# RetNet attention and SwiGLU block: where the attention's first piece, masks and ticks stand in the order of work

## The chip, the core and the metric

The kernel runs on one core of a Trainium2 chip. The core has five engines with queues of their own, each worked off in order: TensorE (PE, matmuls, with its weight loads shown as PEld), VectorE (DVE), ScalarE (ACT), GpSimd (POOL) and SyncE (SP), which here only issues DMAs. The metric is the device time of one execution in microseconds (us). Before the change it is 1050.05 us, the median of six runs from 1048.7 to 1053.18.

## What is computed

Eight batches of eight heads attend over 576 tokens of 64 values each. The scores are scaled, multiplied by a power of a decay per head where the key is not later than the query, and applied to the values, with no softmax. The result, put side by side by heads, is a matrix x of 4608 tokens by 512 that goes through a SwiGLU block. All is float32.

```python
scores = scale * np.matmul(q, k.transpose(0, 1, 3, 2))
Dmat = np.where(rel >= 0, gamma[:, None, None] ** rel[None, :, :], 0.0)
attn = np.matmul(scores * Dmat[None], v)
x = attn.transpose(0, 2, 1, 3).reshape(4608, 512)
g = x @ w_gate                      # 512 -> 1536
out = (g / (1.0 + np.exp(-g)) * (x @ w_val)) @ w_out   # 1536 -> 512
```

## The kernel before, in words

**The block.** The tokens are cut into five tiles: tile 0 of 512 tokens, tiles 1 to 4 of 1024. In tiles 1 to 4 the products are made by a fast scheme with fewer multiplications, written out by hand in the tables `UP`, `DOWN` and `OUT_SUMS` (L50 to L133): 26 products instead of 32. One line of `UP` is one step: sums of blocks of x, sums of blocks of weights, a product, and then reads of the product's bank (copies, sums, and outputs through silu). A tile's up part is three passes over the 26 lines (one for each 512 columns of the hidden layer), each step four matmuls of 128x256; its down part is one pass over the 26 lines of `DOWN`, six matmuls each. `up_step` (L966) and `down_step` (L1019) emit a step; `reads` (L906) emits what follows the matmuls, on DVE where a bank in PSUM is read, on POOL or DVE else. Line 18 of `UP` has six reads, the most of all. In tile 1 the sums of the weights are made too, by POOL (`w_sums`, L945), and stored by ACT's queue (L986); later tiles fetch them again through SP's queue (`fetch`, L875).

**The attention.** A tick t (L673) works on three pairs of heads at once: on PE it emits the values of pair t-2 (`own_values`, L523, and `earlier_values`, L545), the states of pair t-1 (`new_states`, L536) and the scores of pair t-1 (`scores`, L561). The rest of its work, for DVE and ACT, is put into the list `pieces` and handed out between later steps:

- `copies` (L582): even states out of PSUM on ACT; `own` (L578): the mask on the scores, DVE; `pairs` (L587): the mask on the last chunk's scores (`ret_last`, L589, DVE) and the first of the state sums; `odd`, `evens`: the other state sums, DVE.
- `outputs` (`to_x`, L606): the finished values of pair t-2 are copied into x, by ACT for pairs 8 to 19 (`light`, L451), by DVE for others.
- `keys` (L493) scales k, and `scale_q` (L482) scales q, both on ACT; two transposes on DVE make qT and kT of pair t (L489); `next_load` (L1079) then issues the loads of pair t+2 on SP (13 DMAs or fewer).

Where pair t-2 is light, the list is: copies, outputs and own in one piece; then pairs, odd, and evens with keys, one at a time; then qT; then kT with the loads. `part_on` (L733) hands out one of these behind an up step, unless that step or the next has five reads or more (L1016: so behind steps 17 and 18 none). A down step hands out three pieces (`go_on(3)`, L1053), where the three of pairs, odd and evens count as one. A tick first hands out whatever the last one has left.

**The order.** All engines work in the order in which the program emits (L1062). Ticks 0 to 13 belong to tile 0. `spread_tick` (L1135) places the others among the steps. In tile 1 the first up pass has no tick. Among the 52 steps of the other two passes, `merge` (L1056) spreads six ticks (12 to 17) evenly: ahead of steps 0, 9, 17, 26, 35 and 43. Ticks 18 to 21 stand ahead of the down steps 2, 7, 13 and 19 (L1156). Tile 2 has eight ticks and tile 3 four, spread evenly; tile 4 has none.

Of the kernel before, what the change touches and what calls it, by code (L numbers as in the profile page):

```python
# [17 lines left out]
ALU = mybir.AluOpType  # L18
# [136 lines left out]
def kernel(  # L155
# [32 lines left out]
    nc = tc.nc  # L188
# [386 lines left out]
    def masked(i):  # L575
        p, sr, (ret, ret_last, state) = i % HP, last_scores(i), places(i)

        def own():  # L578
            nc.vector.tensor_tensor(out=ret, in0=sc, in1=near[:, 2 * p : 2 * p + 2].unsqueeze(2).to_broadcast([P, 2, NFULL, L]),
                                    op=ALU.mult)  # L580

        def copies():  # L582
            (nc.vector.tensor_copy if vector(i + 1) else nc.scalar.copy)(out=even, in_=z[:, 0])

        odd_states = state[:, 1:].rearrange("p (c r) d -> p c r d", r=2)[:, :, 1]

        def pairs():  # L587

            nc.vector.tensor_tensor(out=ret_last, in0=sr, in1=last_near[:, p], op=ALU.mult)  # L589
            at = odd_states  # L590
            nc.vector.scalar_tensor_tensor(out=at, in0=even, scalar=step[:, p : p + 1], in1=z[:, 1], op0=ALU.mult, op1=ALU.add)

        def odd():
            at = odd_states
            for c in range(1, NFULL):
                nc.vector.scalar_tensor_tensor(out=at[:, c], in0=at[:, c - 1], scalar=step[:, HP + p : HP + p + 1],
                                               in1=at[:, c], op0=ALU.mult, op1=ALU.add)

        def evens():
            at = state[:, 0 : NC - 1].rearrange("p (c r) d -> p c r d", r=2)  # L600
            nc.vector.scalar_tensor_tensor(out=at[:, :, 1], in0=at[:, :, 0], scalar=step[:, p : p + 1], in1=even,
                                           op0=ALU.mult, op1=ALU.add)

        return [copies, own, [pairs, odd, evens]]

    def to_x(i):  # L606
        b, p = divmod(i, HP)
# [65 lines left out]
    def tick(t, lo=HP, hi=NP, spread=False, then=None):  # L673
        go_on(len(pieces))
        if hi == HP:

            if lo <= t - 1 < hi:
                scores(t - 1, True)
                new_states(t - 1)
                pieces.extend(masked(t - 1))  # L680
                go_on(3)
            if lo <= t - 2 < hi:
                own_values(t - 2)
            for f in transposes(t) if lo <= t < hi else ():
                f()
            if t + 1 == HP:
                split(0)
            if lo <= t - 2 < hi:
                earlier_values(t - 2)
                if t == HP:  # L690
                    rounding(2)
                    rounding(3)
                to_x(t - 2)[0]()
            if t + 1 == HP:
                rounding(0)
            return
        if lo <= t - 2 < hi:
            own_values(t - 2)
        if lo <= t - 1 < hi:
            new_states(t - 1)  # L700
        if lo <= t - 2 < hi:
            earlier_values(t - 2)
        if lo <= t - 1 < hi:
            scores(t - 1, t - 2 < lo)
        if lo <= t - 1 < hi and whole(t - 2) and not whole(t - 1):
            decay(slice(0, H), slice(0, H), half[1])
        copies, *masks = masked(t - 1) if lo <= t - 1 < hi else (lambda: None,)
        keys, *new = transposes(t) if lo <= t < hi else (lambda: None,)
        outputs = to_x(t - 2)[0] if lo <= t - 2 < hi else lambda: None
        late = needed(1) - 4 <= t < needed(1) - 2 or light(t - 2)  # L710
        if late and masks:
            own, (pairs, odd, evens) = masks
            pieces.extend([lambda: (copies(), outputs(), own()), [pairs, odd, lambda: (evens(), keys())]])
        elif late:
            pieces.append(lambda: (copies(), outputs(), keys()))
        else:
            pieces.extend([lambda: (copies(), keys()), outputs])
            pieces.extend(masks)
        if then and new:
            pieces.extend(new[:-1])  # L720
            pieces.append(lambda: (new[-1](), then()))
        else:
            pieces.extend(new)
            pieces.extend([then] if then else [])
        if not spread:
            go_on(len(pieces))

    def go_on(n):
        for _ in range(min(n, len(pieces))):
# [236 lines left out]
    def up_step(n, qd, i):  # L966
        label, opens, xslot, _, wslot, _, ops = up[i]
        busy = n == 1
        if qd == 0:
            done = lambda i: X_FIRST + (min(3 * i, 2 * i + 2, i + 6) if busy else i)  # L970
            x_sums(n, done(i), done(i + 1), busy)
        if busy:
            if i > 1:
                w_sums(qd, i)
            w = up_view(qd)(wslot)
        else:
            w = operand()[:, 0:512].rearrange("p (g x) -> p g x", g=2)
        rhs = x_view(n)(xslot)
        b = bank(label, i == 0)
        for gv in range(2):  # L980
            for c in range(2):
                m = nc.tensor.matmul(b[:, gv * TB : (gv + 1) * TB], w[:, gv, ts(c, P)], rhs[:, c, :],  # L982
                                     start=(opens and gv == 0 and c == 0), stop=(c == 1), skip_group_check=True)
        stepped.append(m)
        if busy:
            nc.scalar.dma_start(out=up_ops[qd][i].rearrange("p (g x) -> p g x", g=2), in_=w)  # L986
            if i in (20, 23) and qd + 1 < NQ:
                first_sums(qd + 1, *((0, 2) if i == 20 else (2, 4)))
            if i == 24 and qd + 1 < NQ:
                negated(qd + 1, 1)  # L990
                w_sums(qd + 1, 1)
            if 0 < i < N - 1:
                negated(qd, i + 1)
            if qd + 1 == NQ:
                for _ in range({21: 3, 22: 2, N - 1: 3}.get(i, 0)):
                    fetch()
        else:
            fetch()

        def result(o, src, negative, vector):  # L1000
            s = io[:, (silus[0] % 4) * TB : (silus[0] % 4 + 1) * TB]
            silus[0] += 1
            nc.scalar.activation(out=s, in_=src[:, 0:TB], func=AF.Silu, scale=-1.0 if negative else 1.0)  # L1003
            dst = hid[:, qd, o // 4, o % 4]
            if negative:
                return lambda: nc.vector.scalar_tensor_tensor(out=dst, in0=src[:, TB : 2 * TB], scalar=-1.0, in1=s,  # L1006
                                                              op0=ALU.mult, op1=ALU.mult)
            if vector:
                return lambda: nc.vector.tensor_tensor(out=dst, in0=src[:, TB : 2 * TB], in1=s, op=ALU.mult)
            nc.gpsimd.tensor_tensor(out=dst, in0=src[:, TB : 2 * TB], in1=s, op=ALU.mult)  # L1010

        reads(ops, b, busy, result, i > N // 2)
        if qd + 1 == NQ and i + 1 == N:
            while products:
                products.pop(0)[1]()
        if max(len(line[-1]) for line in up[i : i + 2]) < 5:  # L1016
            part_on()

    def down_step(n, i):  # L1019
# [20 lines left out]
        if n + 1 == NTILE and i + 1 == N:  # L1040
            _, o, a = ops.pop()
            d, t = divmod(int(o), 4)
            at, rows = part[int(a)], starts[n] + t * TB
            assert ops == [["add", a, "b", a]]
            for m, queue in enumerate((nc.sync, nc.scalar)):
                nc.vector.tensor_tensor(out=at[:, ts(m, TB)], in0=b[:, ts(m, TB)], in1=at[:, ts(m, TB)], op=ALU.add)
                queue.dma_start(out=out[rows + m * P : rows + (m + 1) * P, d * TB : (d + 1) * TB], in_=at[:, ts(m, TB)])
            return
        reads(ops, b, False, result)
        at = 2 * (i - (N - 1 - X_FIRST // 2))  # L1050
        if 0 <= at < X_FIRST and n + 1 < NTILE:
# [82 lines left out]

    def spread_tick(t):  # L1135
        tick(t, FIRST, NP, True, lambda: next_load(t))

    ticks = lambda a, b: [lambda t=t: spread_tick(t) for t in range(a, b)]
    for n in range(1, NTILE):
# [10 lines left out]
                                      mybir.DependencyInfo(mybir.DependencyClass.Sync, mybir.DependencyReason.DATA), reason="loads in turn")  # L1150
                    load(FIRST + i // 14)
        downs = [lambda i=i: down_step(n, i) for i in range(N)]
        merge((0.0, ticks(done, cut)), (0.5, ups))
        if n == 1:

            for i, f in reversed(list(zip((2, 7, 13, 19), ticks(cut, upto), strict=True))):  # L1156
                downs.insert(i, f)
            merge((0.5, downs))
        else:
            merge((0.0, ticks(cut, upto)), (0.5, downs))  # L1160
        done = upto

# [29 lines left out]
```

## Time and profile before

| | |
|---|---|
| median of six runs | 1050.05 us (1048.7 to 1053.18) |
| the profiled execution | 1051.12 us, its span 1049.4 us |
| PE, DVE, POOL, ACT busy | 98%, 62%, 38%, 28% of the span |
| tile 1: first up step; first down step | 176.4 us; 327.4 us |
| tile 2, first up step | 412.8 us |
| ticks 14, 15, 16, 17 begin on PE | 253.2, 271.6, 293.3, 309.5 us |
| ticks 18, 19, 20, 21 begin on PE | 332.9, 352.3, 371.9, 389.9 us |

All times within the execution are from the start of the span. A line such as "L489 DVE" is line 489 of the kernel below. A wait "A <- B" is idle time of A that B ended; "issue" is a wait for nothing that the profile shows. Timeline rows give start, duration, engine, line, operation, output<-inputs, shape and count, and in brackets the idle time ahead and what ended it. Equal rows may be merged, and their durations then added or spanned. Rows on windows give, for a stretch, the busy time and the number of instructions of PE, PEld, DVE, ACT and POOL, then the granted clock of PE (1.00 is full), the share of the DMA engines and GB/s.

### The profile page before, as it was taken

To read this page: it belongs to the slowest core of one execution; us is meant where nothing else is said; L and a number is where in the kernel's file an instruction comes from. 1 tells how busy PE (TensorE), PEld (TensorE's weight loads), DVE (VectorE), ACT (ScalarE), POOL (GpSimd) and SP (SyncE) were. 2 spreads that over 40 slices of the span, in tenths; PEclk is the share of its full clock that TensorE was granted. 3 is DMA by queue.
4 is the path that set the end of the run, shared out by engine and by line. 5 is a ranking of instruction groups with operands and counts; after the bars stand their busy time and mean duration, and the time that the engine had idled before them with its cause. 6 is when DMAs were issued, how large, how long until landed. Compare 5 with 4: busy or idle time off the path is not lost.

```text
span 1049.4 us, 21507 instructions
## 1 busy us (share of the span) xinstructions
PE 1030.2 (98%) x8448; PEld 846.3 (81%) x8448; DVE 645.5 (62%) x1063; ACT 294.7 (28%) x646; POOL 401.7 (38%) x347
## 2 busy tenths in 40 slices
PE   6999999999999999999999999999999999999998
PEld 5444555888787888888888888888888888888887
DVE  5668868677668767554467787526376645244644
ACT  4466423242533322132322102223120022231110
POOL 2002367766476016622124048412250483222505
PEclk9999999999999999999999999999999999999999
DMA  9999868776678778755676877445554565555553
GB/s 243 253 276 261 194 201 273 203 208 169 186 206 231 212 194 258 198 149 171 185 205 156 231 176 224 154 141 151 151 180 137 156 193 156 153 151 160 182 161 100
DMA packets 310380, 199.10 MB, mean 190 GB/s; under 512 B 220168, under 2 KB 254984, under 8 KB 310280
## 3 DMA queue, kind: packets, MB, share of 16 engines
q1 hardware_dynamic: 279000, 161.51, 56.0%
q10 hardware_dynamic: 31280, 36.22, 10.2%
q8 instruction: 67, 1.10, 0.4%
q14 instruction: 33, 0.27, 0.1%
HBM read 157.56 MB, written 40.11 MB: 188 GB/s over the span
## 4 chain that ended last, share of the span: by engine, by line
PE 79%; DVE 2%; issue 1%; ACT 0%; DMA 0%; ACTq 0%; DVEq 0%
PE bankC L982 12%; PE bankE L982 12%; PE bankB L982 12%; PE bankA L982 12%; PE bankA L1028 6%; PE bankC L1028 6%; PE bankB L1028 6%; PE bankE L1028 6%; PE outer L531 1%; PE inner L572 1%; PE outer L558 1%; PE inner L542 1%; DVE rest L919 1%; DVE rest L785 0%; DVE arena L1006 0%
## 5 line engine op out<-in xcount | busy, mean ns | idle before, releaser
L919 POOL TENSOR_TENSOR rest<-rest 128x512 f32<-128x512 f32 x65 | 91.7, 1416 | 298.9 <-DVE rest L919 279.9
L1003 ACT ACTIVATE io<-rest 128x256 f32<-128x256 f32 x180 | 74.9, 416 | 320.6 <-DVE rest L919 268.1
L982 PE MATMUL bankC<-rest,arena 128*128 128x256 f32 x544 | 129.0, 380 | 0.0
L982 PE MATMUL bankA<-rest,arena 128*128 128x256 f32 x544 | 128.7, 379 | 0.0
L785 POOL TENSOR_TENSOR arena<-arena 128x512 f32<-128x512 f32 (+1 forms) x72 | 112.1, 1569 | 40.1 <-DMA up<-arena 21.9
L982 PE MATMUL bankE<-rest,arena 128*128 128x256 f32 x512 | 123.2, 384 | 0.6 <-DVE rest L919 0.6
L982 PE MATMUL bankB<-rest,arena 128*128 128x256 f32 x512 | 121.3, 380 | 0.0
L1010 POOL TENSOR_TENSOR arena<-rest,io 128x256 f32<-128x256 f32 x72 | 51.9, 726 | 166.9 <-ACT io L1003 166.9
L982 PEld LDWEIGHTS bankA<-rest,arena 128*128 128x128 f32 x544 | 103.2, 190 | 14.5 <-issue 0.5
L982 PEld LDWEIGHTS bankC<-rest,arena 128*128 128x128 f32 x544 | 102.9, 190 | 14.4 <-POOL arena L785 0.3
L982 PEld LDWEIGHTS bankE<-rest,arena 128*128 128x128 f32 x512 | 97.7, 192 | 15.2 <-DVE rest L919 1.0
L982 PEld LDWEIGHTS bankB<-rest,arena 128*128 128x128 f32 x512 | 97.4, 191 | 13.4
L785 POOL TENSOR_TENSOR rest<-rest 128x256 f32<-128x256 f32 (+1 forms) x66 | 67.6, 1044 | 101.7 <-DVE rest L419 62.0
L919 DVE TENSOR_TENSOR rest<-bankB,rest 128x512 f32<-128x512 f32 x72 | 48.9, 687 | 67.4 <-PE bankB L982 45.1
L919 DVE TENSOR_TENSOR rest<-bankC,rest 128x512 f32<-128x512 f32 x72 | 48.8, 686 | 65.8 <-PE bankC L982 45.9
L919 DVE TENSOR_TENSOR rest<-bankA,rest 128x512 f32<-128x512 f32 x72 | 48.9, 687 | 61.7 <-PE bankA L982 44.3
L919 DVE TENSOR_TENSOR rest<-bankE,rest 128x512 f32<-128x512 f32 x71 | 48.2, 687 | 62.0 <-PE bankE L982 47.0
L1006 DVE SCALAR_TENSOR_TENSOR arena<-rest,io 128x256 f32<-128x256 f32 x84 | 58.2, 695 | 10.9 <-ACT io L1003 10.8
L1028 PE MATMUL bankC<-arena 128*128 128x256 f32 x252 | 59.8, 388 | 0.0
L1028 PE MATMUL bankA<-arena 128*128 128x256 f32 x252 | 58.0, 380 | 1.3 <-DVE arena L785 1.3
L1028 PE MATMUL bankB<-arena 128*128 128x256 f32 x252 | 58.5, 381 | 0.0
L1028 PE MATMUL bankE<-arena 128*128 128x256 f32 x252 | 57.9, 379 | 0.0
(189 smaller groups left out, 1625.5 us busy)
## 6 DMA issues: line engine op xcount, KB each, us to landing
arena<-up SPq DMA_DIRECT2D x234, 256.0 KB, 2.6
arena<-dn SPq DMA_DIRECT2D x104, 384.0 KB, 3.4
up<-arena ACTq DMA_DIRECT2D x78, 256.0 KB, 4.0
dn<-rest SPq DMA_DIRECT2D x78, 128.0 KB, 1.8
out_dram<-rest SPq DMA_DIRECT2D x31, 256.0 KB, 5.3
qk<-in_q_dram SPq DMA_DIRECT2D x108, 72.0 KB, 2.8
qk<-in_k_dram SPq DMA_DIRECT2D x108, 72.0 KB, 2.5
rest<-in_moe_w_out_dram ACTq DMA_DIRECT2D x6, 1024.0 KB, 5.4
```

Of the source, the lines that this page charges most:

```text
L531: m = nc.tensor.matmul(value(i, hl, c), s["v"][rows, at], ret[rows, c % 2 if whole(i) else hl, c // 2], start=start, stop=start, skip_grou ...
L542: nc.tensor.matmul(z[half[hl], r, c], s["kn"][chunk(i, hl, 2 * c + r, i < HP)], s["v"][rows, at], start=True, stop=True, skip_group_check= ...
L558: nc.tensor.matmul(xr[half[hl]] if c + 1 == NC else value(i, hl, c), state[half[hl], c, :], s["qT"][half[hl], column(i, hl, c)], start=Fal ...
L572: nc.tensor.matmul(sc[chunk(i, hl, 2 * c + r)[0], r if whole(i) else hl, c], kT[half[hl], at], qT[half[hl], at], start=True, stop=True, sk ...
L785: eng.tensor_tensor(out=dst, in0=srcs[0], in1=srcs[1], op=ALU.add if op[0] == "add" else ALU.subtract)
L919: eng.tensor_tensor(out=at(op[1]), in0=at(op[2]), in1=at(op[3]), op=ALU.add if op[0] == "add" else ALU.subtract)
L982: m = nc.tensor.matmul(b[:, gv * TB : (gv + 1) * TB], w[:, gv, ts(c, P)], rhs[:, c, :], start=(opens and gv == 0 and c == 0), stop=(c == 1 ...
L1003: nc.scalar.activation(out=s, in_=src[:, 0:TB], func=AF.Silu, scale=-1.0 if negative else 1.0)
L1006: return lambda: nc.vector.scalar_tensor_tensor(out=dst, in0=src[:, TB : 2 * TB], scalar=-1.0, in1=s, op0=ALU.mult, op1=ALU.mult)
L1010: nc.gpsimd.tensor_tensor(out=dst, in0=src[:, TB : 2 * TB], in1=s, op=ALU.mult)
L1028: nc.tensor.matmul(b[:, m * TB : (m + 1) * TB], lhs[:, qd, ts(m, P)], w[:, qd], start=(opens and qd == 0 and m == 0), stop=(qd == NQ - 1), ...
```

## The change

Three things change. `ret_last` leaves `pairs` and becomes a function `last`; in ticks with light values both masks (`own`, `last`) now stand ahead of `outputs`. For ticks from `spread_tick`, the first piece is handed out in the step that follows the tick, between its matmuls and its reads (`after_tick`). And in tile 1 the ticks stand ahead of other steps: 0, 10, 17, 24, 34 and 44 of the two up passes and 4, 8, 14 and 18 of the down part. Tiles 2 and 3 keep their places.

```diff
+        def last():
+            nc.vector.tensor_tensor(out=ret_last, in0=sr, in1=last_near[:, p], op=ALU.mult)
+
         def pairs():
-            nc.vector.tensor_tensor(out=ret_last, in0=sr, in1=last_near[:, p], op=ALU.mult)
             at = odd_states
...
-        return [copies, own, [pairs, odd, evens]]
+        return [copies, own, [last, pairs, odd, evens]]
...
         if late and masks:
-            own, (pairs, odd, evens) = masks
-            pieces.extend([lambda: (copies(), outputs(), own()), [pairs, odd, lambda: (evens(), keys())]])
+            own, (last, pairs, odd, evens) = masks
+            pieces.extend([lambda: (copies(), own(), last(), outputs()), [pairs, odd, lambda: (evens(), keys())]])
         elif late:
             pieces.append(lambda: (copies(), outputs(), keys()))
         else:
             pieces.extend([lambda: (copies(), keys()), outputs])
-            pieces.extend(masks)
+            for own, (last, pairs, *rest_of) in [masks] if masks else []:
+                pieces.extend([own, [lambda: (last(), pairs()), *rest_of]])
...
+    fresh = []
+
+    def after_tick():
+        if fresh:
+            fresh.pop()
+            go_on(1)
...
+        after_tick()
         reads(ops, b, busy, result, i > N // 2)          # up_step
...
+        after_tick()
         reads(ops, b, False, result)                     # down_step
...
     def spread_tick(t):
         tick(t, FIRST, NP, True, lambda: next_load(t))
+        fresh.append(t)
...
-        merge((0.0, ticks(done, cut)), (0.5, ups))
         if n == 1:
-            for i, f in reversed(list(zip((2, 7, 13, 19), ticks(cut, upto), strict=True))):
+            for i, f in reversed(list(zip((0, 10, 17, 24, 34, 44), ticks(done, cut), strict=True))):
+                ups.insert(i, f)
+            merge((0.5, ups))
+            for i, f in reversed(list(zip((4, 8, 14, 18), ticks(cut, upto), strict=True))):
                 downs.insert(i, f)
             merge((0.5, downs))
         else:
+            merge((0.0, ticks(done, cut)), (0.5, ups))
             merge((0.0, ticks(cut, upto)), (0.5, downs))
```

## The prediction

> **What bounds the kernel now.** I read the page first, then the list of waits on TensorE (PE), then the clock in windows of 3.41 us around each wait, and last the timeline and the DMA rows at those places.
>
> ```profile
> span 1049.4 us, 21507 instructions
> PE 1030.2 (98%) x8448; PEld 846.3 (81%) x8448; DVE 645.5 (62%) x1063; ACT 294.7 (28%) x646; POOL 401.7 (38%) x347
> ```
>
> PE is the bound, so only what PE waits for can be won. The columns of the next view are total us, times, longest.
>
> ```profile
> PE inner L572 <- issue: 2.0, 1, 2.0
> PE outer L566 <- DVE kT L489: 1.7, 1, 1.7
> PE bankA L1028 <- DVE arena L785: 1.3, 1, 1.3
> PE bankE L982 <- DVE rest L919: 0.6, 1, 0.6
> ```
>
> All four lie in tile 1, at 337, 275, 366 and 193 us; the other waits in that list fall in tile 0's attention, and from 412 us on there is none. Two of the four cost twice, as windows of activity show (PE busy first, the granted clock after POOL):
>
> ```profile
> 272.66:276.07 3.41, 1.68 (x85) 1.48 (x75) 3.31 (x7) 0.94 (x3) 1.44 (x2) 1.00 0.12 34
> 276.07:279.49 3.42, 3.42 (x9) 2.71 (x9) 0.43 (x1) 0.09 (x2) 0.00 (x0) 0.50 0.99 222
> ...
> 334.10:337.51 3.41, 1.38 (x72) 1.17 (x63) 3.41 (x2) 0.00 (x0) 3.33 (x2) 1.00 0.67 108
> 337.51:340.92 3.41, 3.41 (x11) 2.79 (x9) 1.46 (x1) 0.00 (x0) 3.04 (x2) 0.50 1.08 260
> ...
> 364.82:368.23 3.41, 2.07 (x10) 1.50 (x9) 3.38 (x5) 0.00 (x0) 0.00 (x0) 1.00 0.03 9
> 368.23:371.60 3.37, 3.37 (x17) 2.98 (x16) 2.73 (x4) 0.58 (x1) 0.00 (x0) 1.00 0.82 133
> ```
>
> A window with PE busy 1.68 or 1.38 of 3.41 us is followed by one at clock 0.50, which loses 1.7 us; one with 2.07 us is not. So the wait at 275 cost 1.73 + 1.7 = 3.4 us, that at 337 cost 2.03 + 1.8 = 3.8 us (the step behind it took 4.37 us for the usual 2.59), and that at 366 only 1.3 us. Together 8.5 us: no more can be won here.
>
> **The change part by part.** I write "step" for an up or down step; its PE time is 1.73 us (up) or 2.59 us (down), from the starts in the timeline.
>
> *Tick 15, from step 26 to step 24 (counted from the second pass of tile 1).* Its scores need the kT of tick 14, which a piece of that tick makes. The timeline of before:
>
> ```profile
> 256.47 0.69 DVE L919 TENSOR_TENSOR rest<-bankB,rest 128x512 f32<-128x512 f32 x1 [1.16 <-POOL rest L919]
> ...
> 260.44 2.91 DVE L1006 SCALAR_TENSOR_TENSOR arena<-rest,io 128x256 f32<-128x256 f32 x2
> ...
> 264.69 0.68 DVE L579 TENSOR_TENSOR ret<-inner,near 128x512 f32<-128x512 f32 x1
> ...
> 268.10 1.89 PE L982 MATMUL bankA<-rest,arena 128*128 128x256 f32 x8
> ...
> 273.03 0.77 DVE L489 STREAM_TRANSPOSE qT<-qk 128x576 f32<-128x576 f32 x1
> ...
> 274.31 0.76 DVE L489 STREAM_TRANSPOSE kT<-qk 128x576 f32<-128x576 f32 x1
> ...
> 275.12 0.27 PE L566 MATMUL outer<-qT,kT 64*64 64x64 f32 x2 [1.73 <-DVE kT L489]
> ```
>
> PE ran step 24 at 268.10, tick 15 at 271.64, and wanted kT at 275.12 - 1.73 = 273.39. VectorE (DVE) was some 5 us behind, since steps 18 to 23 read much and each of its SBUF-only operations (L1006) ended only with the POOL sum beside it. Tick 14 stays ahead of step 17. Steps 17 and 18 carry no pieces (step 18 has six reads), so before, the pieces stood behind steps 19 to 24, kT last. After, the first piece is out at step 17 and the rest stand behind 19 to 23: kT moves up by one step. But tick 15 moves up by two. It starts where step 24 did, about 268.15, and wants kT 1.75 us later, at 269.9.
>
> When is kT there? Behind step 23's reads qT ended at 273.80; kT follows it directly, 0.70 later: 274.5. The mask and last mask leave this stretch (0.61 + 0.13, start to start): 273.8. They go where DVE idled before 257.48, but the mask waits for the copy on ScalarE (ACT), which stands behind the silu at 257.20 to 257.61: mask 258.0, last mask 258.6, step 17's read at 258.7 for 257.48: +1.2. DVE's wait of 0.99 for a silu at 272.36 shrinks, as the key scaling stands one step earlier; I take 0.4 of it. So 274.6, a wait of 4.7 us, and a slow window, 1.7: 6.4 against 3.4, **+3.0 us**. Low end: the 1.2 vanishes in waits for POOL and all of the 0.99 goes: 272.8, wait 2.9 and half a slow window 0.9: +0.4. High end: one more L1006 waits out a POOL sum (1.0): 275.6, wait 5.7 and a window and a half, 2.6: +4.9. I take +3.0, the value nearest to the rows.
>
> *Tick 18, from down step 2 to 4.* Its wait is not for an engine: 27 of 30 equal matmuls ran, then 2.03 us nothing. The DMA rows of 334 to 335 us:
>
> ```profile
> q1 hardware_dynamic: 1132, 0.14, 88.4%
> q8 instruction: 1, 0.02, 6.6%
> ```
>
> One packet of instructions of 16 KB (6.6% of 16 engines in 1 us is 1.06 us) travels among 1132 small packets of SyncE's (SP) loads of q and k. I read the wait as PE out of instructions. The loads, of attention tick 19, are issued behind kT of tick 17 (330.87) and take SP from 330.93 to 337.33, over tick 18 at 332.88. After, that kT stands behind step 23, and the loads start 1 to 3 us earlier while tick 18 starts 5.2 us later, at about 338: they no longer meet. **-3.8 us**; the other bound is 0, if PE runs short at another tick. I take -3.8, as the ticks at 293 and 372 us show no such wait. On SP the moved loads (ten DMAs, 6.4 us) also stand ahead of the operands for down steps 5 to 7: issued by 334 and landing in the 6.0 us of the DMA rows there, 340, against down step 5 at about 342.6. If that cover goes, each us late is a us on PE.
>
> *Tick 19, from down step 7 to 8.* The 1.3 us at 366 is down step 11 waiting for the four sums of step 8 (L785, 0.96 each), which stood behind tick 19's DVE work. They now stand ahead of it. But a down step runs three pieces, and with the first already out both transposes follow in the same step, so the sum of step 9, which step 12 needs, stands behind the whole tick: by the same durations it ends near 364 against 363.1 wanted. Late next is step 12, 0.9 us: **-0.4 us**, from -1.3 to +1.0.
>
> *Masks ahead of the copies to x.* In tile 1's down steps the last mask waited for ACT's copies (0.96 us each). Now ACT's copies wait for DVE's masks, and behind them on ACT queue silus, bank copies and key scaling. The next tick writes those banks 10 us later or more, so copies of 1.3 to 1.8 us are hidden; without that cover, about 1 us a tick. ACT is 28% busy. 0. In tile 0 (ticks 10 to 13) a 0.21 us operation moves: 0, within 0.3.
>
> *First piece early in the other ticks.* Ticks 16 and 17 have kT ready 5 steps ahead. At tick 17 the masks fit into DVE's idle 3.04 us before 313.83. In tiles 2 and 3 the piece is copy and key scaling, 1.3 us on ACT, and PE waits for nothing there: 0. The mask build on POOL (1.26 us at 390.27) comes a step earlier into 47 us of POOL idle: 0.
>
> **Sum:** +3.0 - 3.8 - 0.4 = -1.2 us. The profiled execution took 1051.12 us, 1.72 beyond its span; this gives 1049.9. It was 1.07 above the median of the six runs, 1050.05: it fell into both slow windows, which by where a window begins another run can miss. Against the median I see no change. About 0.2% (2.1 us) is what a measurement of this kernel can tell from none.
>
> A rule that speaks here: the Trainium skill, "TensorE: Matmul & The Clock Gate", Part 1, has the clock halve after an idle window of about 3.4 us. The trace differs: 1.7 us idle within a window was enough. By the rule neither wait of before would have cost a slow window, but the new one of 4.7 us could; the sum would be (4.7 + 1.7 - 1.73) - 2.03 - 0.4 = +2.2, an estimate. I go by the rows.
>
> **Rivals.**
>
> Faster: kT is in time. If DVE does not fall 5 us behind, because masks done early let it past steps 18 to 23 without the POOL sums in its way, kT comes by 272: a wait of 2.0, a window 1.7, +0.3. With -3.8 and -1.3 this is 1046.3. For it: 2.9 us of DVE's lag are waits and lock-outs that need not recur. Against: the bare operations from step 18's read at 259.2 on add up to 10.6 us, 269.8, with no wait at all, and POOL is busy until 268.4.
>
> Slower: PE still runs out of instructions once. For it: loads follow each kT directly, ticks 19 and 21 now stand 4 down steps behind the tick whose pieces issue them, and loads of before crossed ticks 17 and 19 unharmed, so that the meeting alone does not decide. At the same 3.8 us the sum is +3.0 - 0.4 = +2.6: 1053.7; it turns the sign from a loss of 2.3 us on, a stop long enough to bring a slow window. Against: one tick out of ten was hit before, and the worst meeting is taken apart.
>
> Slower by tick 15 alone: kT after 276.8 (wait 6.9, window 1.7) is where it outweighs the rest; at 277.2, 1052.6, with a second slow window 1053.5.
>
> The change does not do what it says: the early piece waits for the scores anyway and DVE orders the rest as before, so each wait comes back at its size, 1051.
>
> **How the numbers follow.** Trade of one wait for another, as summed: 0.32. Does nothing: 0.07. Faster: 0.26, widened beyond what the sum gives since the largest term rests on a queue of DVE that I moved by hand. Instructions late: 0.22. Tick 15 alone: 0.13. So within 0.2%: 0.39, faster 0.26, slower 0.35. Predicted 1049.9, its own range 1048 to 1052. The range over the cases reaches from 1045.9, below the faster case, to 1054.0, above the dearest of the slower ones.
>
> **What would show it.** Right: a wait of PE for kT at the scores of tick 15 near 270, longer than 1.73, and a window at clock 0.50 behind it; no wait for "issue" at a tick of the down steps; a short wait at down step 12. Wrong: no wait for kT (then faster), an "issue" wait at any tick (then slower), any wait beyond 412 us.

## The result, and the profile after

The changed kernel takes 1052.14 us in the median of 35 runs (1049.25 to 1057.2), against 1049.07 us for 77 runs of the kernel before, run in turn with it. The ratio is 1.0031, 95% interval 1.002 to 1.0042: slower by about 3 us. A second comparison gave 1.0029 (1.0017 to 1.0042). The prediction was 1049.9 us, with "Against the median I see no change".

The profiled execution took 1051.01 us, almost the 1051.12 of before, so these two profiles taken alone would show no loss. The page of the changed kernel:

```profile
span 1049.3 us, 21500 instructions
PE 1028.1 (98%) x8448; PEld 843.8 (80%) x8448; DVE 654.4 (62%) x1063; ACT 297.6 (28%) x646; POOL 401.3 (38%) x347
```

The list of waits on PE of the changed kernel (total us, times, longest). Lines have moved by 10 behind the new functions: L929 is the old L919, L992 the old L982, L795 the old L785, L1039 the old L1028.

```profile
PE outer L566 <- DVE kT L489: 3.1, 1, 3.1
PE inner L542 <- ACT kn L506: 1.5, 2, 1.3
PE bankC L992 <- DVE rest L929: 1.4, 1, 1.4
...
PE bankE L992 <- DVE rest L929: 1.0, 1, 1.0
PE outer L558 <- DVE state L603: 1.0, 1, 1.0
...
PE bankB L1039 <- issue: 0.2, 1, 0.2
```

The two waits of before in the down part are gone (2.03 us of "issue" at tick 18, 1.3 us at down step 11). The 0.20 us of "issue" left there stand at down step 12 (369.03 us) and are a wait for DVE: a sum (L795) that step 12 needs ended at 368.93. At tick 15, 1.73 us became 1.29 us for the scaled keys kn and 3.11 us for kT. New and not predicted is the 1.4 us for bankC, at step 24 of the third up pass (329 us). The 1.0 us for bankE lies in the first pass, where before had 0.6.

The timeline at tick 15 of the changed kernel (start, duration, engine, line, operation, output<-inputs, shape, count, idle time ahead):

```profile
256.64 0.69 DVE L579 TENSOR_TENSOR ret<-inner,near 128x512 f32<-128x512 f32 x1 [1.62 <-ACT even L583]
257.25 0.21 DVE L588 TENSOR_TENSOR ret_last<-outer,last_near 128x64 f32<-128x64 f32 x1
...
258.06 0.69 DVE L929 TENSOR_TENSOR rest<-bankA,rest 128x512 f32<-128x512 f32 x1 [0.59 <-PE bankA L992]
...
265.15 2.75 DVE L598 SCALAR_TENSOR_TENSOR state<-state,tab 128x64 f32<-128x64 f32 x3
...
270.06 1.08 PE L542 MATMUL inner<-v,kn 64*64 64x64 f32 x29 [1.29 <-ACT kn L506]
...
271.34 0.78 DVE L489 STREAM_TRANSPOSE qT<-qk 128x576 f32<-128x576 f32 x1 [0.58 <-ACT qk L486]
...
274.29 0.77 DVE L489 STREAM_TRANSPOSE kT<-qk 128x576 f32<-128x576 f32 x1
...
275.11 0.37 PE L566 MATMUL outer<-qT,kT 64*64 64x64 f32 x2 [3.11 <-DVE kT L489]
```

The masks do stand early, in DVE's idle time, as the first two rows show. But kT ends at 275.06, where it ended before too (274.31 + 0.76), while PE, held up by kn first, asked for it at 272.00 instead of 273.39. The three `odd` sums of 128x64 take 2.75 us from first start to last end, for 1.50 before: the last two take 1.19 us each, and each ends 0.08 us after a sum of POOL that ran beside it.

Windows of 3.41 us there and at the wait in the third pass (PE, PEld, DVE, ACT, POOL busy with counts, PE's clock, DMA share, GB/s):

```profile
268.71:272.12 3.41, 1.88 (x89) 1.54 (x84) 2.83 (x7) 3.20 (x9) 0.00 (x0) 1.00 0.42 147
272.12:275.53 3.41, 0.42 (x14) 0.42 (x18) 2.94 (x4) 0.42 (x1) 2.67 (x2) 0.50 0.27 88
275.53:278.95 3.42, 3.42 (x38) 2.85 (x33) 0.82 (x2) 1.51 (x5) 0.00 (x0) 0.50 0.67 109
...
326.73:330.14 3.41, 1.97 (x10) 1.44 (x9) 3.41 (x6) 1.47 (x4) 0.98 (x1) 1.00 0.79 297
```

Two windows at clock 0.50 stand at tick 15 in this execution. The first falls mostly on idle time; the second is full of work at half speed.

To compare kernels I cut tile 1 in two, by starts in the timeline: "up" from the first up step of tile 1 to its first down step, "down" from there to the first up step of tile 2. Tiles 2 to 4 take 636.6 to 637.5 us in every profile of this study, so nothing changed there.

| profile | up | down | sum | profiled execution |
|---|---|---|---|---|
| before | 151.05 | 85.32 | 236.37 | 1051.12 |
| before_2 | 149.25 | 83.64 | 232.89 | 1045.22 |
| before_3 | 151.68 | 85.33 | 237.01 | 1051.12 |
| after | 156.60 | 79.96 | 236.56 | 1051.01 |
| after_2 | 156.14 | 79.96 | 236.10 | 1051.8 |
| after_3 | 156.84 | 79.95 | 236.79 | 1056.74 |
| after_4 | 158.92 | 79.97 | 238.89 | 1056.98 |

By the means, with after_4 left out of the up part (4.14 us of it are a wait at 196 us, told of below), the up part lost 5.9 us and the down part gained 4.8. The first of the three up passes has no tick, and its waits differ from profile to profile, from 0.3 to 4.1 us. The other two passes together take 102.7 to 105.2 us in the profiles of before (mean 104.3) and 108.0 to 110.9 us in the four of the changed kernel (mean 109.6).

### The profile page after: what moved, and what is told of

It reads as the page before. It is cut to its first block, busy times and chain, and to the rows that moved or that the text cites. A ratio compares the mean times of both kernels' runs of the same rounds, so it can differ in the third digit from the quotient of the medians.

```text
span 1049.3 us, 21500 instructions
## 1 busy us (share of the span) xinstructions
PE 1028.1 (98%) x8448; PEld 843.8 (80%) x8448; DVE 654.4 (62%) x1063; ACT 297.6 (28%) x646; POOL 401.3 (38%) x347
## 4 chain that ended last, share of the span: by engine, by line
PE 79%; DVE 2%; issue 0%; DMA 0%; ACT 0%; POOL 0%; ACTq 0%; DVEq 0%; POOLq 0%
PE bankC L992 13%; PE bankE L992 12%; PE bankA L992 12%; PE bankB L992 12%; PE bankB L1039 7%; PE bankC L1039 6%; PE bankE L1039 6%; PE bankA L1039 6%; PE outer L531 1%; PE inner L572 1%; DVE rest L929 1%; PE outer L558 1%; PE inner L542 1%; DVE state L598 1%; DVE arena L1016 0%
## 5 line engine op out<-in xcount | busy, mean ns | idle before, releaser
L929 POOL TENSOR_TENSOR rest<-rest 128x512 f32<-128x512 f32 x65 | 91.9, 1418 | 297.4 <-DVE rest L929 276.3
L992 PE MATMUL bankC<-rest,arena 128*128 128x256 f32 x544 | 129.0, 380 | 1.6 <-DVE rest L929 1.4
L992 PE MATMUL bankA<-rest,arena 128*128 128x256 f32 x544 | 130.0, 382 | 0.0
L795 POOL TENSOR_TENSOR arena<-arena 128x512 f32<-128x512 f32 (+1 forms) x72 | 112.5, 1575 | 45.5 <-DMA up<-arena 30.1
L992 PE MATMUL bankE<-rest,arena 128*128 128x256 f32 x512 | 121.4, 380 | 1.0 <-DVE rest L929 1.0
L992 PE MATMUL bankB<-rest,arena 128*128 128x256 f32 x512 | 121.3, 380 | 0.0
L992 PEld LDWEIGHTS bankC<-rest,arena 128*128 128x128 f32 x544 | 102.9, 190 | 16.6 <-issue 1.8
L992 PEld LDWEIGHTS bankA<-rest,arena 128*128 128x128 f32 x544 | 104.1, 192 | 14.9 <-issue 0.5
L992 PEld LDWEIGHTS bankE<-rest,arena 128*128 128x128 f32 x512 | 97.0, 190 | 14.7 <-DVE rest L929 1.4
L992 PEld LDWEIGHTS bankB<-rest,arena 128*128 128x128 f32 x512 | 96.9, 190 | 13.4 <-issue 0.2
L795 POOL TENSOR_TENSOR rest<-rest 128x256 f32<-128x256 f32 (+1 forms) x66 | 66.9, 1035 | 101.2 <-DVE rest L419 61.2
L929 DVE TENSOR_TENSOR rest<-bankC,rest 128x512 f32<-128x512 f32 x72 | 48.9, 688 | 64.7 <-PE bankC L992 45.7
L929 DVE TENSOR_TENSOR rest<-bankB,rest 128x512 f32<-128x512 f32 x72 | 48.8, 686 | 62.9 <-PE bankB L992 48.6
L929 DVE TENSOR_TENSOR rest<-bankA,rest 128x512 f32<-128x512 f32 x72 | 48.9, 687 | 62.4 <-PE bankA L992 45.1
L929 DVE TENSOR_TENSOR rest<-bankE,rest 128x512 f32<-128x512 f32 x71 | 48.2, 688 | 63.3 <-PE bankE L992 49.3
L1016 DVE SCALAR_TENSOR_TENSOR arena<-rest,io 128x256 f32<-128x256 f32 x84 | 56.0, 667 | 10.9 <-ACT io L1013 10.9
L1039 PE MATMUL bankB<-arena 128*128 128x256 f32 x252 | 58.3, 381 | 0.0
L1039 PE MATMUL bankC<-arena 128*128 128x256 f32 x252 | 58.1, 380 | 0.0
L1039 PE MATMUL bankA<-arena 128*128 128x256 f32 x252 | 57.9, 379 | 0.0
L1039 PE MATMUL bankE<-arena 128*128 128x256 f32 x252 | 57.9, 379 | 0.0
```

What stands on the lines that cost most here:

```text
L795: eng.tensor_tensor(out=dst, in0=srcs[0], in1=srcs[1], op=ALU.add if op[0] == "add" else ALU.subtract)
L929: eng.tensor_tensor(out=at(op[1]), in0=at(op[2]), in1=at(op[3]), op=ALU.add if op[0] == "add" else ALU.subtract)
L1039: nc.tensor.matmul(b[:, m * TB : (m + 1) * TB], lhs[:, qd, ts(m, P)], w[:, qd], start=(opens and qd == 0 and m == 0), stop=(qd == NQ - 1), ...
```

## The experiments

Two theories stood at first. One: tick 15's place, two steps earlier, carries the loss. Its rival: the pieces (early first piece, masks ahead) lose time wherever they run, and the place is a detail. A third came up on the way: that the order of the masks costs in tile 0.

**Tick 15 back to step 26, the rest of the change kept.**

```diff
-(0, 10, 17, 24, 34, 44), ticks(done, cut)
+(0, 10, 17, 26, 34, 44), ticks(done, cut)
```

> The changed kernel with one number undone: tick 15 ahead of step 26 again, not 24. Theory (the place of tick 15 is the loss: it leaves no step between the transposes of tick 14 and the scores that need them): the waits of 1.3 and 3.1 us at tick 15 shrink to under 1 us together, no or one slow window instead of two, so 5 to 7 us less than the changed kernel, ratio to the kernel before 0.996 to 0.999. Rival (the early piece pushes VectorE's reads of steps 17 and 18 back): the changed kernel's loss stays, 1.002 to 1.003.

Ratio to before 0.9992 (0.9973 to 1.0012); up 150.37, down 79.96. Its waits on PE in the second and third pass:

```profile
PE bankC L992 <- DVE rest L929: 1.5, 1, 1.5
PE bankA L992 <- DVE rest L929: 0.9, 1, 0.9
PE outer L566 <- DVE kT L489: 0.5, 1, 0.5
```

One number takes the whole loss away. The wait for kT falls to 0.51 us, for the 1.73 of before at the same place. But 0.87 us of that is PE coming later, by a wait for bankA ahead of the tick: together 1.39 us for 1.73.

**Tick 15 at step 25.** The same line with 25.

> The changed kernel with tick 15 ahead of step 25, half of the way back (24 gave an up stretch of 156.6 us, 26 gave 150.4). Theory (time of kT is fixed by VectorE, each step that tick 15 comes earlier is 1.73 us more of waiting): waits at tick 15 of 2.5 to 3 us together, one slow window, up stretch 152.5 to 154.5. Rival (a threshold, the transposes find a free queue or not): as with 24 or as with 26, within 0.7 us.

Up 152.06, down 79.98, one execution of 1051.98 us.

```profile
PE outer L566 <- DVE kT L489: 2.2, 1, 2.2
...
PE bankC L992 <- DVE rest L929: 1.4, 1, 1.4
PE bankA L992 <- DVE rest L929: 0.9, 1, 0.9
```

At steps 24, 25 and 26 the waits for kn and kT together are 4.40, 2.23 and 0.51 us; with the 0.9 us for bankA, which stands ahead of the tick at steps 25 and 26, they are 4.40, 3.09 and 1.39. That is 1.3 to 2.2 us for each step, around the PE time of one up step, 1.73: the wait is set by the place. At step 25 no slow window followed, where one had been expected. The 1.4 us for bankC is there at all three.

**Only the places, without the early piece and with the old order of the masks.** The last hunk of the diff, applied to the kernel before.

> The ticks at the new places, but the pieces as before (no early piece, masks behind the copies). Theory: kT of tick 14 is then not even handed out when tick 15 comes and is flushed there, so tick 15 waits as long as in the changed kernel or up to 1.7 us longer; ratio 1.003 to 1.005. Rival (the early piece is the loss): 1.000 or below.

Ratio 1.001 (0.9994 to 1.0026); up 155.81, down 81.03. The waits at tick 15 are 1.38 us for kn and 0.85 for kT, with two windows at clock 0.50, and no wait at step 24 of the third pass. The ratio of 1.003 or more that was expected did not come. In the first pass, where no tick stands, 2.9 us are waits.

**Only the pieces, at the old places.** The other hunks, with the ticks at 0, 9, 17, 26, 35, 43 and 2, 7, 13, 19.

> The early piece and the masks ahead of the copies, but the ticks at the places of before. Theory: kT of tick 14 stands behind step 23 and tick 15 ahead of step 26, two steps apart: its wait falls from 1.7 to under 0.5 us and its slow window goes; ratio 0.996 to 0.999. Rival (the early piece is the loss): 1.002 to 1.003, with VectorE's reads of steps 17 to 19 late and a wait for them on TensorE of 1 us or more in either pass.

Ratio 0.9999 (0.998 to 1.0017); up 151.15, down 80.90. No stop of 2 us for "issue" comes although tick 18 stands at down step 2 as before; 1.44 us at step 24 of the third pass is there. At tick 15 PE waits 1.52 us for bankA and then 0.51 for kT, 2.0 in all for the 1.73 of before: the early piece shifted this wait and did not take it away. A short stop for "issue" stands in the midst of equal matmuls behind tick 21:

```profile
394.07 1.13 PE L1039 MATMUL bankC<-arena 128*128 128x256 f32 x4 [0.62 <-issue]
```

So most of the down part's gain can be had by the pieces alone, or by the places alone (81.03). The up part's loss needs both: the second and third pass together take 106.8 us with the places alone and 105.2 with the pieces alone, for 104.3 before and 109.6 with both.

**The ticks of the up part further apart.**

```diff
-(0, 10, 17, 24, 34, 44), ticks(done, cut)
+(0, 8, 15, 27, 36, 45), ticks(done, cut)
```

> The changed kernel with the up ticks ahead of steps 0, 8, 15, 27, 36 and 45: tick 14 two steps ahead of the heavy line 18 and tick 15 eight steps behind it, tick 17 behind the heavy line. Theory: the transposes are three steps or more ahead of the scores at every tick, so no wait over 0.5 us at a tick of tile 1 and no slow window; 7 to 9 us below the changed kernel, ratio to before 0.994 to 0.997. Rival (VectorE is late whatever the places): a wait of 1 us or more stays, 0.999 to 1.002.

Ratio 0.9998 (0.9981 to 1.0014); up 153.07, down 80.00. No wait for kT is left; other waits came up, 1.64 us for DVE's reads in the first pass, 1.30 for POOL's sums near 271 us and 0.91 in the third pass, so the expected 0.994 to 0.997 was missed.

**The two kernels again, unchanged.** Is the 2.03 us of "issue" an accident of one execution, and how far does tile 1 vary?

> The kernel before once more, for a second profile. I compare stretches: from the first up step of tile 1 to its first down step (151.1 us in the first profile), from there to tile 2 (85.3 us). Theory: the 2.0 us stop without a cause at tick 18 was an accident of that execution and no property of the place, so the down stretch is about 81.5 us, and the up stretch stays within 1.8 us of 151.1 with the wait for kT of 1.7 us. Rival: the stop belongs to the place of tick 18, and the down stretch is 85 again.

> The same a third time, with the same expectations: theory 81.5 us for the down stretch, rival 85.

> The changed kernel once more. Theory (tick 15's wait is set by VectorE and two slow windows follow): up stretch of tile 1 155 to 158 us against 149.3 to 151.7 before, down stretch 80.0 against 83.6 to 85.3. Rival (the two slow windows were an accident): up stretch 152.5 to 154. For tile 0, theory that tick 13's wait for the states there comes with the changed code: 0.5 to 2 us at 165; rival: chance, none.

> The changed kernel a third time, with the same expectations: theory an up stretch of 155 to 158 us and a wait of 0.5 to 2 us at tick 13 in tile 0, rival 152.5 to 154 and no such wait.

The stop of 2.03 us stands at the same matmul in all three profiles of before and in none of after. Where I had expected an accident, that fell. In before_2 no window from 60 us on ran at clock 0.50, with waits of 1.51 and 2.03 us: its windows happen to start elsewhere, so that PE is busy 1.90 and 1.96 us of the two, and the execution took 1045.22 us. The changed kernel's waits, 1.28 to 1.29, 3.11 and 1.44, came back in every profile. In after_3 a wait of 3.27 us for the states in tile 0 (168 us) with two windows at 0.50 was added.

**The masks behind the copies to x again.**

```diff
-pieces.extend([lambda: (copies(), own(), last(), outputs()), [pairs, odd, lambda: (evens(), keys())]])
+pieces.extend([lambda: (copies(), outputs(), own()), [lambda: (last(), pairs()), odd, lambda: (evens(), keys())]])
```

> The changed kernel with the masks behind the copies to x again; the early piece and the places stay. Theory (the order of masks and copies moves only ACT's copies and a 0.2 us operation): up stretch as in the changed kernel within 1 us, down stretch within 1 us of 80. Rival (VectorE is freed by it in the down part, 1 us a tick): the down stretch comes back to 81 or more with a wait at step 11 or 12; in tile 0 the wait for the states at tick 13 goes.

Up 157.60, down 79.52, 1054.55 us; waits at tick 15 of 1.43 and 3.11, at step 24 of the third pass 1.52. In this one profile tile 1 does not care for the order of the masks; clear18_mb, below, agrees.

**No early piece.** `fresh.append(t)` left out.

> The changed kernel without the early piece; the masks ahead of the copies and the places stay. Tick 15 then stands ahead of step 24 with kT not yet handed out. Theory: the wait of 1.4 us at step 24 of the third pass goes, as the state sums fall behind the two reads of step 21 again; tick 15 waits as long as in the changed kernel or longer: up stretch 154.5 to 158. Rival (the early piece itself is what makes VectorE late at tick 15): up stretch 153 or less.

Up 154.27, down 84.27, 1052.87 us. Two lines of its timeline, in the third pass, and then the same two operations in the changed kernel with the matmul that waited:

```profile
324.24 1.27 DVE L929 TENSOR_TENSOR rest<-bankC,rest 128x512 f32<-128x512 f32 x2
325.44 3.32 DVE L598 SCALAR_TENSOR_TENSOR state<-state,tab 128x64 f32<-128x64 f32 x3
```

```profile
324.50 3.30 DVE L598 SCALAR_TENSOR_TENSOR state<-state,tab 128x64 f32<-128x64 f32 x3
...
327.72 1.28 DVE L929 TENSOR_TENSOR rest<-bankC,rest 128x512 f32<-128x512 f32 x2
...
329.14 1.97 PE L992 MATMUL bankC<-rest,arena 128*128 128x256 f32 x8 [1.44 <-DVE rest L929]
```

This is the unforeseen 1.44 us. The early piece moves `odd` of tick 17 one step forward, ahead of the reads of step 21. Three small sums last 3.3 us beside POOL's sums, the reads come that much later, and step 24, which writes the same bank, waits. Without the early piece the reads go first and no such wait stands there.

In the down part the early piece earns its keep: without it PE waits 1.04 us at down step 3 and 1.61 us at down step 12. The list of waits puts both down to ACT's copies of the banks, but these had ended at 340.01 and 369.55 us, and PE went on at 340.43 and 370.54. What ended just ahead of that is a sum of DVE (L795), at 340.33 and 370.44, for which a semaphore instruction in PE's queue waited. At step 12 the chain begins at the masks: ACT's copies to x waited 3.27 us for the last mask, the scaling of q came behind them, qT waited 1.78 us for that, and the sum came behind qT. That is the work by which the prediction's "hidden" copies would cost.

**Ticks where their pieces have room.** Tick 14 ahead of step 11 rather than 17, so that its pieces are done before the crowded step 18; tick 15 at 23.

```diff
-(0, 10, 17, 24, 34, 44), ticks(done, cut)
+(0, 4, 11, 23, 34, 49), ticks(done, cut)
```

> The changed kernel with the up ticks ahead of steps 0, 4, 11, 23, 34 and 49: all pieces of a tick are out before line 18 in the second pass, and tick 17 stands behind line 18 in the third. Theory (waits come where pieces and the six reads of line 18 meet on VectorE): no wait of TensorE over 0.5 us from the first tick to tile 2, up stretch 146 to 148, down stretch 80; ratio to before 0.994 to 0.997. Rival (VectorE is late there by the reads and POOL's sums alone): waits of 1 us or more stay at steps 22 to 24, up stretch 149 or more, ratio 0.998 or more.

Ratio to before 0.9958 (0.994 to 0.9975), where the changed kernel has 1.0031; up 148.37, down 80.52. Between 140 and 420 us these waits are left:

```profile
PE bankE L992 <- DVE rest L929: 0.8, 1, 0.8
PE bankB L1039 <- issue: 0.5, 2, 0.3
```

The two of "issue" stand at down steps 3 and 12 and end with a sum of DVE, as above. kT of tick 14 is done at 255.5 us, 13.1 us after its tick began on PE, and tick 15 asks for it 12 us later. In the changed kernel it took 21.3 us from the tick, and tick 15 came 14.5 us behind it. Tick 15 stands a step earlier here than in the changed kernel: early it may be, if tick 14 is earlier still.

**Tile 0.** In the profiles so far PE waited near 165 us for the states in eight of nine kernels or repeats with the masks ahead (0.3 to 3.3 us), and in one of five with the masks behind. This looked like the missing part of the loss. Four runs on one chip, the first with the old order in ticks of tile 0 alone:

```diff
+if not spread:
+    pieces.extend([lambda: (copies(), outputs(), own()), [lambda: (last(), pairs()), odd, lambda: (evens(), keys())]])
+else:
     pieces.extend([lambda: (copies(), own(), last(), outputs()), [pairs, odd, lambda: (evens(), keys())]])
```

> The changed kernel, but in tile 0's ticks the masks stand behind the copies to x again. Theory: the order of the masks makes tile 0's last wait for the states (0.3 to 3.3 us near 165 us, and with the longer ones a slow window). Then that wait is gone (under 0.3 us), the profile's tile 1 stays at 156 + 80 us, and the ratio to the kernel before falls from 1.0031 to 1.000 to 1.0015. Rival: the wait comes from out_sums on DVE ahead of the state sums, whose own wait differs from run to run, and the order has no part in it: the wait stays at 0.5 us or more, and the ratio at 1.002 to 1.004.

> The changed kernel once more, beside the others on the same chip. Every theory: ratio to the kernel before 1.002 to 1.004; waits of 1.29 and 3.11 us at tick 15 and 1.44 us at step 24 of the third pass. The theory on tile 0 wants a wait of 0.3 us or more near 165 us here and none in the run with the masks behind; the rival sees none or one in both.

mb_tile0 1.0028 (1.0012 to 1.0044), the changed kernel 1.0029 (1.0017 to 1.0042). With the old order in tile 0 the wait stayed, 1.21 us at 165 us; clear18_mb and clear_old, with the old order too, waited there 1.05 and 1.99 us.

The theory on tile 0 fell. The order of the masks there is worth nothing that these runs can tell (the two intervals leave about 2 us either way). The wait differs from execution to execution, and so does the seam to tile 1: after_4 had 4.14 us at 196 us, behind sums of DVE that had waited 2.93 us for stores of `dn`; in no other profile is a wait there longer than 1.64 us.

**The best places with the masks behind, and with nothing but the places.** Both with up steps 0, 4, 11, 23, 34, 49 and down steps 4, 8, 14, 18; the second without the early piece and with the old masks.

> The ticks at up steps 0, 4, 11, 23, 34, 49, and the masks behind the copies to x in every tick. Theory: the places and the early piece carry the gain, the order of the masks only costs in tile 0: up 148 to 150 us, down 80 to 81 us, no wait for states near 165 us, ratio to the kernel before 0.993 to 0.996, at or below the same places with the masks ahead (0.9958). Rival: masks ahead help where the ticks have room: waits for the states or scores come up in tile 1, ratio 0.997 or more.

> The kernel before in all but the places: ticks at up steps 0, 4, 11, 23, 34, 49 and down steps 4, 8, 14, 18, no early piece, masks behind. Theory: the places alone make the up part short (148 to 150 us); without the early piece the waits of the down part stay near 84 us as in the run without it (84.3), so the ratio to the kernel before is 0.995 to 0.998. Rival: the early piece is needed for the up part too (154 us as in the run without it): ratio 0.999 to 1.002.

clear18_mb: 0.9954 (0.9939 to 0.9968), up 149.48, down 79.84, as with the masks ahead. clear_old: 0.9997 (0.9982 to 1.0011), up 148.70, down 83.48. The places alone make the up part short; but in the down part PE stops at down step 3:

```profile
338.71 0.94 DVE L785 TENSOR_TENSOR rest<-arena 128x768 f32<-128x768 f32 x1
...
339.75 2.67 PE L1028 MATMUL bankB<-arena,rest 128*128 128x256 f32 x6 [2.03 <-issue]
```

The size and the word are those of the stop of before, to the hundredth, but it is another thing. This matmul reads `rest`, and the semaphore instruction ahead of it in PE's queue waited for the sum of DVE in the first line, which ended at 339.65. That sum stood behind three state sums of 128x64, drawn out to 1.83 to 1.86 us each beside sums of POOL. PE waits for the same sum, 1.04 us, in no_early and in places_only: all three kernels with the new places in the down part and no early piece wait 1 us or more at this step. Here the window with the wait had PE busy 1.38 us, and one at 0.50 followed.

## Why the prediction was wrong

**Tick 15, "+3.0 us" with bounds "+0.4" and "+4.9": mis-sized, and this decides.** The reading was right, its numbers nearly so: kT at 275.06 for "274.6", a wait of 4.40 (1.29 for kn, 3.11 for kT) for "4.7". The masks came 1.4 us earlier than worked out, which did not help, since `odd` beside POOL took 2.75 us and one step's sum and products (272.04 to 274.3) still stood between qT and kT. Two things were missed. First, the slow windows: this term of the sum was too small by them. "1.73+1.7" against "4.7+1.7" takes one window each; in profiles of the same tile 1 (after, after_2, after_3, mb_tile0) there were 2, 1, 2 and 1 (after_4, whose up part has the 4.14 us besides, had none), in those of before 1, 0 and 1 at tick 15. By means that is 1.5 against 0.67 windows, +1.4 us. Second, the wait of 1.44 us at step 24 of the third pass, which is not tick 15's, see the next point. Tick 15's own term is then +4.1 (waits +2.7, windows +1.4) for "+3.0"; with the third pass it makes +5.5; the up part measured 156.4 (mean of those four; 155.90 in mb_tile0) less 150.7 (mean of three), +5.7.

**"First piece early in the other ticks", put at 0: this step failed.** "At tick 17 the masks fit into DVE's idle 3.04 us" is true (the mask starts at 317.69 in 1.20 us of idle time), but a piece handed out early moves every later piece of the tick forward too, and I followed the first only. `odd` at 324.50 put step 21's reads off; 1.44 us in every kernel with the early piece and tick 17 at step 43 or 44, none in no_early, places_only and before.

**Tick 18, "-3.8 us": the size is right, the reading right in one half.** The stop took 2.03 us and its slow window 1.7, and neither is in the changed kernel. In before:

```profile
334.58 0.63 PE L572 MATMUL inner<-qT,kT 64*64 64x64 f32 x27
337.24 0.33 PE L572 MATMUL inner<-qT,kT 64*64 64x64 f32 x3 [2.03 <-issue]
```

"PE out of instructions" is borne out. In the 18 profiles PE stops 19 times for more than 0.06 us ahead of a matmul that waits for no semaphore. Each time 449, 705, 6849 or 8129 records of its queue (matmuls, weight loads and semaphore instructions) had begun, and these numbers lie whole multiples of 256 apart. The 0.62 us of pieces_only is among the 19; the 2.03 us of clear_old is not. The queue q8, of kind "instruction", brings 67 packets of 16 KB for 17298 such records, one for 258, and at each of the 19 stops PE went on 1.3 to 1.7 us after such a packet had landed (in before at 337.24, the packet at 335.73). In before the 256 records ahead of the stop are small matmuls of tick 18 alone, and PE was through them in 2.26 us (332.95 to 335.21), ahead of that landing. In the changed kernel the 256 records ahead of the same place begin with down steps (41 records, 338.50 to 343.1 us) and take 6.3 us, and the packet lands 2.3 us ahead of the need.

"Behind SP's loads" is not borne out. The packet travelled 1.05, 1.54 and 0.88 us in the three profiles of before; 0.88 is as short as any of the 1206 on record, and the stop was 2.03 us all the same. pieces_only runs the 256 records in 1.98 us, while SP issues the same loads (331.5 to 339.3 us), without a stop: there the packet set out 1.65 us ahead of them, in the profiles of before 1.2 to 1.9 us behind their start. What makes a packet set out early or late stays open.

**Tick 19, "-0.4 us": mis-sized, on the good side.** The 1.34 us at down step 11 are gone, and the "short wait at down step 12" came, 0.20 us for the "0.9": the sum stood behind both transposes, as forecast. That makes -1.1 us. The down part in all fell from 84.8 (mean of three) to 79.96, -4.8 for "-4.2".

**The base.** The sum was made against an execution with both windows, 1051.12 us, and the median of the before runs is 1049.1 to 1050.4, its lowest 1044.0. In before a slow window comes or does not, by where a window begins: of the 5.9 us between before_2 (1045.22) and before (1051.12), the two slow windows of tile 1 are 3.4. The prediction said that "another run can miss" the windows, and yet counted them as won in full: -1.8 of the -3.8. In the changed kernel the wait of 4.4 us brought a slow window in four of the five profiles, and no run fell below 1049.25.

**What stays open.** By the means of tile 1 the change costs about 1 us (+5.7 - 4.8), where the prediction had -1.2; the timed comparisons say 3. Tick 15's place accounts for the loss in time: with it undone the ratio is 0.9992. But without that place tile 1 is 5 us shorter than before by the profiles (230.3 for a mean of 235.4), and the ratio of t15_back shows a gain of 0.8, at best 2.8. What is missing stands ahead of tile 1. From tile 0's first up matmul to tile 1 the three profiles of before take 146.4 to 147.3 us, the four of the changed kernel 148.1 to 153.2 and t15_back 151.3 (a wait of 1.82 us for the states near 166 us and a slow window of 1.7 behind it); of the 15 profiles of kernels other than before, 14 take longer than 147.3. The order of the masks there does not decide it: mb_tile0 takes 148.6, and places_only and clear_old, whose tile 0 is written as in before, 148.9 and 152.7. Why tile 0 is longer in these profiles, and whether three of before are enough to say so, stays open.

**The rivals.** "Faster: kT is in time" missed by 3 us of kT: the POOL sums were in the way of DVE again. "Slower by tick 15 alone" asked for kT after 276.8; it came at 275.06, and tick 15's place turned the sign all the same. (By its own numbers that sum is wrong: a kT at 275.8 already outweighs the rest, 5.9 + 1.7 - 3.4 = 4.2, and a second window of 1.7 on 1052.6 gives 1054.3, not 1053.5.) "PE still runs out of instructions once" was not seen in the four profiles of the changed kernel from 23 us on; pieces_only, with 0.62 us, shows that it can happen. "Masks ahead of the copies to x", put at 0, held.

**The rule of the Trainium skill**, "TensorE: Matmul & The Clock Gate", Part 1, that the clock halves after an idle window of about 3.4 us, is again not what the rows show: windows with PE busy 1.38 to 1.70 us were followed by clock 0.50. Its sum, +2.2, lies nearer to the result than mine, but by a mechanism that before_2 against before_3 contradicts: there waits below 2.1 us made or did not make a slow window.

## What to carry to other kernels

When a piece of work is handed out a step earlier, follow every later piece of the same list past the reads it now precedes, not the first alone. A producer's place matters as much as its consumer's: moving tick 14 out of the crowded steps took away a wait that moving tick 15 had only shifted. Two waits of one size need not be one thing: look at what ended just ahead of each. Before a gain is booked that hangs on a clock window, take more than one profile of the kernel before.

## What the runs showed of the hardware

- Between 60 us and the end of the matmuls, windows of 3.41 us with PE busy 1.70 us or less were followed by one at clock 0.50 in every case but one (after_4, 1.63 us). Windows at full clock with 1.78 to 1.99 us mostly were not, but twice they were (1.88 in after, 1.90 in places_only). The very last window of work is different: with 1.44 to 1.54 us busy no slow window is on record behind it. A second slow window could follow a first in which PE was busy (1.81 and 2.86 us in after_3, 3.27 in clear_old). So the border is not sharp in these records. Where a window begins differs from run to run, and one wait of 1.5 to 2 us costs 0 or 1.7 us more by it.
- State sums of 128x64 on DVE, from SBUF to SBUF, take 0.28 us with POOL idle (clear18) and up to 1.86 us beside a POOL sum (clear_old, 1.83 to 1.86 for each of three).
- PE can run out of instructions. All 19 of its stops over 0.06 us that no semaphore explains stand at one of four places in its queue that lie multiples of 256 records apart, and last 0.08 to 2.03 us. Numbered in order, one packet of q8 to each such place from the 449th record on (66 in each of 18 profiles), PE never went past one sooner than 1.28 us after its packet had landed. PE ran 256 records of small matmuls (64x64) in 2.0 to 2.3 us (pieces_only, before); the stop behind them in before and before_3 was followed by a slow window.
